# A transformer block on one core: four more units with a joint maximum step, value products and projections at other steps

## The chip, the cores and the metric

The kernel runs on one core of a Trainium2 chip. A core has five engines, each with its own instruction stream and working in order: TensorE (PE in the profile; PEld are its weight loads), VectorE (DVE), ScalarE (ACT), GpSimd (POOL) and SyncE (SP), which here only issues transfers. They meet through semaphores. Matrix products land in PSUM, eight banks of 128 partitions x 512 fp32 values, from which DVE and ACT read.

The metric is the device time of one execution in microseconds (us), as the median over several runs. A separate, profiled execution gives the trace.

## The reference

A layer-normed multi-head attention block, followed by a layer-normed gated feed-forward block, each with its residual. One sequence of 2048 tokens, width 512, 32 heads of 16, feed-forward width 1792, bf16 inputs.

```python
x = A_x                                              # 1 x 2048 x 512
h = x + A_ref(layernorm(x), A_wqkv, A_wo)
h2 = h + B_ref(layernorm(h), B_w_gate, B_w_up, B_w_down)

def A_ref(x, wqkv, wo):                              # H = 32, Dh = 16
    q, k, v = split_heads(x @ wqkv)
    scores = einsum("bhqd,bhkd->bhqk", q, k) * Dh ** -0.5
    p = softmax(scores, axis=-1)
    return merge_heads(einsum("bhqk,bhkd->bhqd", p, v)) @ wo

def B_ref(x, w_gate, w_up, w_down):
    return (gelu_tanh(x @ w_gate) * (x @ w_up)) @ w_down
```

The softmax needs the maximum of each of the 32 x 2048 rows of 2048 scores before the exponentials.

## The kernel before, in words

**Units and steps.** Attention is cut into 64 units: 8 groups of 256 queries (`gi`), and in each 8 slots of 4 heads. A unit's index is `ui`; units 8g to 8g+7 are group g. The schedule is written out by a planner in Python that runs through steps (`tick` in the code), 16 to a unit. Everything below is recorded into one list per engine, in the planner's order; the engines then run these lists, held up only by semaphores.

**First pass, for the maxima.** In each step PE computes two score tiles of 128 queries x 512 keys, of two heads (`p1_pair`, matmuls at line 825, 32 rows high since a head has 16 values and some room for the maximum), into a pair of PSUM banks. DVE reduces the pair to its maxima in one instruction over 128 x 1024 values (`p1_consume`, line 840, into `PM`). Two pairs of banks take turns. At the end of a unit POOL combines the maxima (`negm_part`, `negm_pre`), splits the negated maximum into three bf16 parts, SP transposes them (`STG`), and POOL adds them into the query tile `QT` (line 888), so that the second pass's scores come out with the maximum already taken off.

**Joint units.** In the units listed in `JOINT` two of the first pass's steps become one. For two heads, `item_diff` has PE compute the scores of the fourth block of 512 keys less those of the third (lines 1022 and 1024, the second with negated queries `QN` that POOL makes at line 1014), and ACT keeps the positive part (a Relu, line 1027, into `RB`, which shares the space of `OA`). At step 10 of the unit DVE adds this to the third block's scores and takes the maximum, with one instruction for each of the two heads (line 837): max(s3, s4) = s3 + max(s4 - s3, 0). Step 14 (`J_GONE`) then has nothing left to do and is left out altogether, for the second pass too, whose two tiles per step are made up for by a third tile in odd steps (`behind`).

**Second pass, for the probabilities.** It runs 24 steps behind the first (`P2_START`). In each step PE computes two tiles of 128 keys x 256 queries, twice (line 904), and ACT turns each 512 columns of PSUM into bf16 exponentials (`p2_consume`, line 933) in a ring of 34 tiles (`PTM`, `PTE`, `PTG`). It uses the banks 4 to 7, which it shares with the dense work. After the last step of the first pass the second goes on alone, two tiles to one ACT instruction (line 921).

**Dense work.** One queue (`Dense`) holds everything else that PE does, a piece in each step, behind the step's scores:
- `item_pv`: the products of the exponentials with the values, 64 matmuls a unit (line 947), in four pieces. A piece may start no earlier than its step in the unit's second pass; the list `PV_T` gives the first step, and in the kernel before the other three are `4 * p + 5`, so that they stand at 13, 14, 15 and 17. Then ACT copies the result (`OB`, line 669), SP transposes it, and POOL inverts the sums and multiplies (lines 981 and 985) into `Otok`.
- `post_onT` and `item_oproj`: when all slots of a group are done, SP transposes `Otok` into `OnT` (line 1067), PE projects it (line 1087) and adds the residual, ACT copies with a sum (line 1094), a Square with a sum follows (`sq`, line 1101), POOL finishes the layer norm, and SP transposes the result (`post_hnT`, line 1077). `clear` lets both transposes start in a window of a unit's steps only.
- `item_gate`, `item_up`, `item_down`: the feed-forward of 256 tokens: 7 pairs of gate and up, each with an ACT copy (line 669), a tanh on ACT (line 1148) and six POOL instructions, and two output projections of 14 matmuls (line 1220) and one for the residual (line 1225).

Where a step has too little dense work the planner fills with matmuls whose result nobody reads (`dummy`, line 1380). The planner keeps an account of how far ACT is behind (`act_lag`), and starts gate and up, output projections, difference items (`LAG_EXTRA`) and the Square (`LAG_OP`) only while it is small.

**The end.** The feed-forward of the last group can only follow the last attention unit (`tail_b`). There DVE takes over copies from ACT, and what dense work is left is put into waits (`fill`) or in front of the last feed-forward.

Of the kernel before, what the change touches and what calls it, by code (L numbers as in the profile page):

```python
# [218 lines left out]

NPT_M, NPT_E, NPT_G = 23, 4, 7  # L220
NPT = NPT_M + NPT_E + NPT_G
PV_T = (13, 14, 16, 17)
ADDX = 3
LAGX = 8
PAUSE = 1
# [4 lines left out]
LAG_OP = 0.2  # L230
TANH_LAG = 2
SLOPE = 0.02
JOINT = (12, 14, 17, 20, 25, 28, 33, 36, 41, 44, 49)
J_AT, J_GONE = 10, 14
LAG_EXTRA = 0.2
POLY = 1.3
TICK = 1.135
TOOK = {1.04: 1.13, 0.62: 0.7, 1.27: 1.26, 1.45: 1.67, 0.31: 0.4}
# [3 lines left out]
def bass_sequential_preLN__mha_block__geglu_ffn__prompt_kernel(nc, A_x, A_wqkv, A_wo, B_x, B_w_gate, B_w_up, B_w_down, out):  # L242
    dbg = None
    with ExitStack() as es:
# [268 lines left out]
        def startable(it, room):  # L513
            if it[0] is item_gate and par_busy[it[1][1] % 2] and room < 10:
                return False
            if it[0] is item_down and it[1] == (GL - 1, 1) and not force[0]:
                return False
            if it[0] is item_down and not force[0] and (tight() or dense.now // 16 in JOINT and dense.now % 16 > J_GONE - 6 or act_lag[0] > LAG_START):
                return False
# [4 lines left out]
        class Dense:  # L524
# [27 lines left out]
            def piece(self):  # L552
                if self.single and self.pause > 0:
                    return 0
                while True:
                    if self.gen is None:
# [6 lines left out]
                        elif self.prio and (not self.single or self.prio[0][3] <= self.now):  # L563
                            self._start(self.prio.pop(0))
                        elif self.extra and not tight() and act_lag[0] <= LAG_EXTRA and self.now + 2 <= lim and not (self.ready and self.ready[0][0] is item_up):
                            self._start(self.extra.pop(0))
# [26 lines left out]
        dense = Dense()  # L593
        behind = [0]
        def tight():
            return dense.now // 16 in JOINT and dense.now % 16 >= J_GONE - 2 or bool(behind[0])

        deferred = []
        def defer(k, fn):
            deferred.append((dense.now + k, fn))  # L600
        force = [False]
# [47 lines left out]
        act_lag = [0.0]  # L649
        def act_more(cost):  # L650
            act_lag[0] += cost
# [179 lines left out]
        def p1_consume(ui, tiles):  # L831
            par = ui % 2
            (b, qt, kc, g), (b2, _, _, g2) = tiles
            if ui in JOINT and (qt, kc, g) == (1, 2, 0):
                assert y_left[ui] == 0, "differences too late"
# [7 lines left out]
        def negm_part(ui, k):  # L843
# [10 lines left out]
            else:  # L854
# [3 lines left out]
                P.op("pool", lambda e: e.tensor_scalar(out=m3, in0=m3, scalar1=-1.0, scalar2=None, op0=ALU.mult), reads=[("MXm", par)], writes=[("MXm", par)])  # L858
                if ui in JOINT:
                    P.op("pool", lambda e: e.tensor_copy(out=PM[:, par, 1, 3, 0:2], in_=PM[:, par, 1, 2, 0:2]), reads=[("PM", par, 1, 2, g_) for g_ in (0, 1)], writes=[("PM", par, 1, 3, g_) for g_ in (0, 1)])  # L860
# [75 lines left out]
        def item_pv(b, ui):  # L936

            gi, slot = units[ui]
            for p in range(4):
                while not force[0] and dense.now < P2_START + 16 * ui + 4 * p + 5:  # L940
                    yield ("wait", 1)
                for m in (2 * p, 2 * p + 1):
                    for i in range(2):
                        kt = 2 * m + i
                        for g in range(4):
                            pi = pt_of[(ui, m, g)]
                            P.op("pe", lambda e, g=g, kt=kt, pi=pi, i=i: e.matmul(pbank[32 * g:32 * g + 17, b, 0:256], VA[:, kt, 4 * slot + g, :],  # L947
                                                                                  PTt(pi)[:, 256 * i:256 * i + 256], start=(kt == 0), stop=(kt == NT - 1), tile_position=(0, 32 * g)),
                                 reads=[("V", kt), "VA_ones", ("PT", pi)], writes=[("pb", b)], sig=(g == 3 and i == 1))
                    for g in range(4):  # L950
                        pt_busy.discard(pt_of.pop((ui, m, g)))
                if p < 3:
                    yield 2
            par, col = slot // 2 % 2, slot % 2
            if gi == GL and slot >= NSLOT - 2:
                evac_act(OA[:, par, 256 * col:256 * col + 256], pbank[:, b, 0:256], [("pb", b)], [("OA", par, col), ("RB", 1)], cost=0.27)
                if col == 0:
                    dense.add(item_ofin, gi, front=True, est=3, not_before=dense.now + 3)
            else:
                evac_act(OB[:, ui % 2, :], pbank[:, b, 0:256], [("pb", b)], [("OB", ui % 2)], cost=0.27, then=lambda: o_turn(ui))  # L960
            pv_done.add(ui)
            return 2

        pv_done = set()
        P2_START = 16 + LAGX

        ob_busy = {}
        def o_turn(ui):
            gi, slot = units[ui]
            par = ui % 2  # L970
            assert not ob_busy.get(par), "GpSimd too far behind"
            ob_busy[par] = True
            P.dma("sp", lambda e: e.dma_start_transpose(out=OBT[:, par, :, :], in_=OB[:, par, :]), ("obT", par), reads=[("OB", par)], writes=[("OBT", par)])
            o4 = OBT[:, par].rearrange("p q (g i) -> p q g i", i=32)
            defer(5, lambda: o_norm(gi, slot, par, o4, ("OBT", par), ob_busy))
# [25 lines left out]
            yield  # L1001

        def clear(fn):
            if not force[0] and not 5 <= dense.now % 16 <= 14:
                defer(1, lambda: clear(fn))
            else:
                fn()
# [36 lines left out]
        def add_ffn(gi):  # L1044
            for f in range(NFC // 2):
                dense.add(item_gate, gi, f, est=3)
                dense.add(item_up, gi, f, est=3)
            for k in range(2):
                dense.add(item_down, gi, k, est=5)

        def add_ffn_when(gi):
            if w_pieces or not qkv_over[0]:
                defer(1, lambda: add_ffn_when(gi))
            else:
                add_ffn(gi)
# [7 lines left out]
        def post_onT(gi, k):  # L1063
            gp = gi % 2
            if k == 0:
                load_xres(gi)
            P.dma("sp", lambda e: e.dma_start_transpose(out=OnT[:, k, :, :], in_=Otok[:, k, :]),
                  ("onT", k), reads=[("Otok", s_) for s_ in range(NSLOT)], writes=[("OH", k)])
            if k == 1:
                otok_consumed[gi] = True  # L1070
            dense.add(item_oproj, gi, k, front=True, est=3, not_before=dense.now + 4)

        hn_left = {}
        ffn_done = {}
        def post_hnT(gi, k):
            gp = gi % 2
            P.dma("sp", lambda e: e.dma_start_transpose(out=hnT_l[gp][:, :, 128 * k:128 * k + 128], in_=hn_sb[:, k, :]),
                  ("hnT", 2 * gp + k), reads=[("OH", k)], writes=[("hnT", gp, k)])
            hn_left[gi] = hn_left.get(gi, 2) - 1
            if hn_left[gi] == 0:  # L1080
                defer(3, lambda: add_ffn_when(gi))

        def item_oproj(b, gi, k):
            gp, t = gi % 2, 2 * gi + k
            hh = g_h(gi, k)
            for hc in range(4):
                P.op("pe", lambda e, hc=hc: e.matmul(pbank[:, b, :], OnT[:, k, hc, :], wo_sb[:, hc, :], start=(hc == 0), stop=False),
                     reads=[("OH", k), "wo"], writes=[("pb", b)], sig=False)
                if hc == 1:
                    yield 2  # L1090
            P.op("pe", lambda e: e.matmul(pbank[:, b, :], ident[:], hh, start=False, stop=True),
                 reads=["ident", ("h", gp, k)], writes=[("pb", b)], sig=True)
            act_more(0.48)
            P.op("act", lambda e: e.activation(out=hh, in_=pbank[:, b, :], func=ACT.Copy, accum_out=hsum[:, t:t + 1]),
                 reads=[("pb", b)], writes=[("h", gp, k), ("hsum", t)])
            def sq():
                if not force[0] and act_lag[0] > LAG_OP:
                    defer(1, sq)
                    return
                act_more(0.48)  # L1100
                P.op("act", lambda e: e.activation(out=hn_sb[:, k, :], in_=hh, func=ACT.Square, accum_out=hsq[:, t:t + 1]),  # L1101
                     reads=[("h", gp, k)], writes=[("OH", k), ("hsq", t)])
                defer(1, lambda: pool.add(ln2_from_sums(gi, k, t), then=lambda: defer(2, lambda: clear(lambda: post_hnT(gi, k)))))
            defer(2, sq)
            return 3
# [287 lines left out]
        tick = 0  # L1393
        J_ = sorted(JOINT)
        J_PREP = {max(160, 16 * (J_[i - 1] if i else 0) + 12): J_[i] for i in range(len(J_))}
# [7 lines left out]
        while True:  # L1403
            p1_ok = tick < 16 * NU
            if p1_ok and tick // 16 in JOINT and tick % 16 == J_GONE:
                for i, (k_, fn_) in enumerate(deferred):
# [68 lines left out]
            if p2_ok and t2 % 16 == 0:  # L1475
                dense.add(item_pv, t2 // 16, front=True, est=5, not_before=tick + PV_T[0])
            if doubles[0]:
# [61 lines left out]
```

## Time and profile before

| | |
|---|---|
| time, median of 3 runs | 1240.03 us (1239.23 to 1241.87) |
| time of the profiled execution | 1240.23 us |
| its span, first to last instruction | 1238.5 us |
| PE busy | 1099.2 us |
| DVE busy | 1182.2 us |
| ACT busy | 1196.3 us |
| POOL busy | 785.3 us |
| mean granted clock of TensorE | 0.997 |
| DVE maxima, 128 x 1024 (line 840) | 1002 of 1213 ns each |
| exponentials, 512 columns (line 933) | 2000, about 704 ns each |

The first pass takes from 14.7 to 1183.1 us of the span, the second alone to 1206.9, the end the rest. A duration in such a table is that of one instruction from its start to its end. Instructions of one engine overlap a little, so that the distance from one start to the next can be shorter than the duration.

### The profile page before, as it was taken

How to read it: one execution, taken by the hardware profiler on the slowest of the kernel's cores; microseconds unless marked ns; L12 is line 12 of the kernel's file. 1: busy time of each engine (PE TensorE's matmuls, PEld its weight loads, DVE VectorE, ACT ScalarE, POOL GpSimd, SP SyncE). 2: the span in 40 equal slices, each digit the busy share in tenths (PEclk: the TensorE clock that was granted, in tenths of full speed). 3: DMA queues.
4: the chain of work that ended last, by engine and by line, in shares of the span. 5: the costliest groups of instructions: out<-in, count | busy, mean ns of one | idle time of the engine just before them, and what ended most of it. 6: DMA issues, size and time to landing. Idle time of an engine off the chain costs nothing.

```text
span 1238.5 us, 31200 instructions
## 1 busy us (share of the span) xinstructions
PE 1099.2 (89%) x12389; PEld 429.3 (35%) x12588; DVE 1182.2 (95%) x1111; ACT 1196.3 (97%) x2433; POOL 785.3 (63%) x1624
## 2 busy tenths in 40 slices
PE   7898888888888999889988999989988898888888
PEld 3232222233333333333333333333333333323345
DVE  8999999999999999999999999999999999999933
ACT  7899999999999999999999999999999999999992
POOL 8555884455756467674667638574676847865781
PEclk9999999999999999999999999999999999999999
DMA  5111113400010001000010100100001000010000
GB/s 151 27 30 25 30 27 108 117 10 8 10 25 17 14 12 23 16 15 17 8 27 12 14 17 8 27 16 15 12 10 30 12 18 8 7 32 20 8 15 18
DMA packets 68656, 31.52 MB, mean 25 GB/s; under 512 B 53920, under 2 KB 67488, under 8 KB 68512
## 3 DMA queue, kind: packets, MB, share of 16 engines
q1 hardware_dynamic: 68512, 29.52, 9.9%
q8 instruction: 101, 1.65, 0.6%
q14 instruction: 43, 0.35, 0.1%
HBM read 11.80 MB, written 2.10 MB: 11 GB/s over the span
## 4 chain that ended last, share of the span: by engine, by line
ACT 59%; DVE 30%; PE 8%; issue 1%; POOL 1%; DMA 1%
ACT PTM L933 33%; DVE PM L840 29%; ACT PTG L933 10%; ACT PTE L933 6%; PE pbank L1220 2%; ACT th_sb L1148 2%; ACT u_sb L669 2%; ACT g_sb L669 1%; PE pbank L825 1%; ACT PTM L921 1%; PE pbank L904 1%; PE pbank L1380 1%; PE pbank L1168 1%; ACT OB L669 1%; ACT OnT L1101 1%
## 5 line engine op out<-in xcount | busy, mean ns | idle before, releaser
L840 DVE TENSOR_REDUCE PM<-pbank 128x2 f32<-128x1024 f32 x1002 | 1141.9, 1213 | 11.3 <-PE pbank L904 7.4
L933 ACT ACTIVATE PTM<-pbank 128x512 bf16<-128x512 f32 x1357 | 727.4, 704 | 6.6 <-PE pbank L904 2.0
L904 PE MATMUL pbank<-QT,KT 32*128 32x256 bf16 x4096 | 517.6, 273 | 17.8 <-ACT PTM L933 6.5
L825 PE MATMUL pbank<-KT,QT 32*128 32x512 bf16 x2026 | 390.5, 384 | 25.3 <-DVE PM L840 10.7
L1380 PE MATMUL pbank<-ones_bf,ident 128*128 128x512 bf16 x639 | 206.0, 384 | 65.0 <-ACT PTM L933 31.9
L933 ACT ACTIVATE PTG<-pbank 128x512 bf16<-128x512 f32 x407 | 227.6, 704 | 1.2
L825 PEld LDWEIGHTS pbank<-KT,QT 32*128 32x128 bf16 x2026 | 98.7, 91 | 367.6 <-DVE PM L840 134.4
L904 PEld LDWEIGHTS pbank<-QT,KT 32*128 32x128 bf16 x4096 | 171.5, 92 | 90.4 <-ACT PTM L933 47.2
L933 ACT ACTIVATE PTE<-pbank 128x512 bf16<-128x512 f32 x236 | 137.3, 700 | 0.6
L947 PE MATMUL pbank<-PTM,VA 128*17 128x256 bf16 x2776 | 126.0, 274 | 5.2 <-ACT PTG L933 1.1
L981 POOL TENSOR_TENSOR LINV<-OBT,negone 128x8 f32<-128x8 bf16 x62 | 103.4, 1667 | 0.0
L1380 PEld LDWEIGHTS pbank<-ones_bf,ident 128*128 128x128 bf16 x804 | 46.2, 97 | 137.4 <-ACT PTM L933 90.8
L947 PEld LDWEIGHTS pbank<-PTM,VA 128*17 128x17 bf16 x2776 | 59.9, 89 | 49.7 <-issue 29.8
L1158 POOL TENSOR_TENSOR th_sb<-g_sb 128x512 f32<-128x512 f32 x49 | 50.9, 1039 | 34.9 <-ACT g_sb L669 34.9
L868 POOL TENSOR_TENSOR MX<-PM,MX 128x8 f32<-128x8 f32 x64 | 12.8, 200 | 92.7 <-DVE PM L840 92.1
L1168 PE MATMUL pbank<-hnT_l,wg_sb 128*128 128x256 bf16 x448 | 66.6, 274 | 2.8 <-ACT PTG L933 0.2
L1168 PE MATMUL pbank<-hnT_l,wu_sb 128*128 128x256 bf16 x448 | 66.5, 275 | 2.8 <-ACT PTM L933 0.2
L888 POOL TENSOR_TENSOR QT<-QT,STG 128x256 bf16<-128x256 bf16 x64 | 42.7, 668 | 35.0 <-DMA STG<-ST 35.0
L1157 POOL TENSOR_TENSOR th_sb<-th_sb,g_sb 128x512 f32<-128x512 f32 x49 | 62.1, 1267 | 3.2
L1160 POOL TENSOR_TENSOR th_sb<-th_sb,g_sb 128x512 f32<-128x512 f32 x49 | 62.1, 1267 | 2.9
L1212 POOL TENSOR_TENSOR GUT<-th_sb,u_sb 128x512 bf16<-128x512 f32 x49 | 62.1, 1267 | 2.0
L855 POOL TENSOR_TENSOR MX<-PM,MX 128x8 f32<-128x8 f32 x64 | 12.9, 201 | 74.8 <-DVE PM L840 74.0
(164 smaller groups left out, 1138.6 us busy)
## 6 DMA issues: line engine op xcount, KB each, us to landing
QKS<-QKS SPq DMA_DIRECT2D x27, 112.0 KB, 2.1
x_sb<-in_A_x_dram SPq DMA_DIRECT2D x4, 512.0 KB, 5.6
xres<-in_A_x_dram SPq DMA_DIRECT2D x16, 128.0 KB, 2.3
out_dram<-out_sb SPq DMA_DIRECT2D x16, 128.0 KB, 1.7
wg_sb<-in_B_w_gate_dram SPq DMA_DIRECT2D x4, 448.0 KB, 4.0
wu_sb<-in_B_w_up_dram SPq DMA_DIRECT2D x4, 448.0 KB, 3.9
wd_sb<-in_B_w_down_dram SPq DMA_DIRECT2D x3, 512.0 KB, 5.0
STG<-ST SPq DMA_TRANSPOSE x64, 2.3
```

Source lines behind the costliest of these rows:

```text
L825: P.op("pe", lambda e, g=g, b=b: e.matmul(pbank[:, b, :], QT[32 * g:32 * g + 32, c, slot, 128 * qt:128 * qt + 128], KT[32 * g:32 * g + 32, ...
L840: P.op("dve", lambda e: e.tensor_reduce(out=PM[:, par, qt, kc, g:g + 2], in_=pbank[:, b:b + 2, :], axis=AX.X, op=ALU.max), reads=[("pb", b ...
L904: P.op("pe", lambda e, kt=kt, i=i: e.matmul(pbank[:, b, 256 * i:256 * i + 256], KT[32 * g:32 * g + 32, slot, 128 * kt:128 * kt + 128], QT[ ...
L933: P.op("act", lambda e, b=b, pi=pi: e.activation(out=PTt(pi), in_=pbank[:, b, :], func=ACT.Exp), reads=[("pb", b)], writes=[("PT", pi)], e ...
L947: P.op("pe", lambda e, g=g, kt=kt, pi=pi, i=i: e.matmul(pbank[32 * g:32 * g + 17, b, 0:256], VA[:, kt, 4 * slot + g, :], PTt(pi)[:, 256 * ...
L981: P.op("pool", lambda e: e.tensor_tensor(out=li, in0=o4[:, :, :, 16], in1=negone[:, 0:8].rearrange("p (q h) -> p q h", q=2), op=ALU.pow), ...
L1157: o(1.27, lambda e: e.tensor_tensor(out=ts_, in0=ts_, in1=gs, op=ALU.mult), [("th", par), ("g", par)])], then=done)
L1158: pool.add([o(1.04, lambda e: e.tensor_tensor(out=ts_, in0=gs, in1=gs, op=ALU.mult), [("g", par)], dE), o(0.62, lambda e: e.tensor_scalar( ...
L1160: o(1.27, lambda e: e.tensor_tensor(out=ts_, in0=ts_, in1=gs, op=ALU.mult), [("th", par), ("g", par)])], then=poly_done)
L1168: P.op("pe", lambda e, dc=dc, fc=fc, i=i: e.matmul(pbank[:, b, 256 * i:256 * i + 256], w[:, dc, 128 * fc:128 * fc + 128], hT[:, dc, :], st ...
L1212: P.op("pool", lambda e: e.tensor_tensor(out=o_ap, in0=shp(ts_), in1=shp(us), op=ALU.mult), reads=[("th", par), ("u", par)], writes=o_keys ...
L1380: P.op("pe", lambda e: e.matmul(pbank[:, b, :], ident[:], ones_bf[:, 0:512], start=True, stop=True), reads=["ident", "ones_bf"], writes=[( ...
```

## The change

1. `JOINT` has 15 units instead of 11: unit 12 goes, 11, 22, 30, 38 and 46 come.
2. The four pieces of the value products take their steps from `PV_T`, 15, 16, 17 and 18.
3. The window in which `clear` lets the transposes start ends at step 13 instead of 14.
4. `item_oproj` may start 5 steps after its transpose is issued instead of 4.
5. The feed-forward of a group is added 4 steps after its last transpose instead of 3.
6. The Square waits while a gate or up item is under way and ACT's account with it would be over the limit.
7. `LAG_EXTRA`, up to which a difference item may start, is 0.3 instead of 0.2.

The computation is the same.

```diff
-PV_T = (13, 14, 16, 17)
+PV_T = (15, 16, 17, 18)
...
-JOINT = (12, 14, 17, 20, 25, 28, 33, 36, 41, 44, 49)
+JOINT = (11, 14, 17, 20, 22, 25, 28, 30, 33, 36, 38, 41, 44, 46, 49)
 J_AT, J_GONE = 10, 14
-LAG_EXTRA = 0.2
+LAG_EXTRA = 0.3
...
             for p in range(4):
-                while not force[0] and dense.now < P2_START + 16 * ui + 4 * p + 5:
+                while not force[0] and dense.now < P2_START + 16 * ui + PV_T[p]:
                     yield ("wait", 1)
...
         def clear(fn):
-            if not force[0] and not 5 <= dense.now % 16 <= 14:
+            if not force[0] and not 5 <= dense.now % 16 <= 13:
                 defer(1, lambda: clear(fn))
...
-            dense.add(item_oproj, gi, k, front=True, est=3, not_before=dense.now + 4)
+            dense.add(item_oproj, gi, k, front=True, est=3, not_before=dense.now + 5)
...
-                defer(3, lambda: add_ffn_when(gi))
+                defer(4, lambda: add_ffn_when(gi))
...
             def sq():
-                if not force[0] and act_lag[0] > LAG_OP:
+                if not force[0] and act_lag[0] + (0.48 if dense.gen is not None and dense.cur in (item_gate, item_up) else 0) > LAG_OP:
                     defer(1, sq)
                     return
```

## The prediction

> **What bounds the kernel now.** I read the page's busy shares first, then the chain of waits.
>
> ```profile
> PE 1099.2 (89%) x12389; PEld 429.3 (35%) x12588; DVE 1182.2 (95%) x1111; ACT 1196.3 (97%) x2433; POOL 785.3 (63%) x1624
> ...
> ACT 59%; DVE 30%; PE 8%; issue 1%; POOL 1%; DMA 1%
> ```
>
> DVE and ACT are both nearly always busy and the chain changes between them, so neither line names the pace. "Busy" counts an instruction until it has left the engine, and successive ones overlap; the pace is the distance from start to start. The timeline of DVE around a joint step, then of ACT:
>
> ```profile
> 673.56 9.33 DVE L840 TENSOR_REDUCE PM<-pbank 128x2 f32<-128x1024 f32 x8 [0.21 <-PE pbank L904]
> 682.81 0.68 DVE L837 CUSTOM_DVE_ANT_0 OA<-pbank,OA 128x512 f32<-128x512 f32 x1
> ...
> 684.03 5.78 DVE L840 TENSOR_REDUCE PM<-pbank 128x2 f32<-128x1024 f32 x5
> ```
>
> ```profile
> 526.06 1.27 ACT L933 ACTIVATE PTG<-pbank 128x512 bf16<-128x512 f32 x2
> 527.01 0.81 ACT L669 ACTIVATE u_sb<-pbank 128x512 f32<-128x512 f32 x1
> 527.49 2.29 ACT L933 ACTIVATE PTM<-pbank 128x512 bf16<-128x512 f32 x4
> ```
>
> A plain DVE step is 1.131 us (the usual start-to-start distance of L840; its lasting 1.213 hides 0.08 of idling), the joint step 684.03 - 682.81 = 1.22. An exponential, or any 512-column copy from PSUM, holds ACT 0.477 us (526.06 to 527.01 is two); a tanh 0.52, the 256-column OB copy 0.264, a Square with its sum read 0.61, an oproj copy with its sum read 0.57. The windows show DVE alone setting the time, stretch by stretch:
>
> ```profile
> core 0: us, PE busy (x) PEld busy (x) DVE busy (x) ACT busy (x) POOL busy (x), PEclk, DMA share, GB/s
> 110.67:219.27 108.60, 92.15 (x1090) 30.83 (x1106) 108.60 (x98) 107.23 (x216) 73.45 (x130) 1.00 0.20 57
> 633.35:778.55 145.20, 131.41 (x1510) 50.94 (x1534) 143.81 (x133) 144.60 (x300) 93.44 (x198) 1.00 0.08 16
> 671.02:688.59 17.57, 15.64 (x181) 5.93 (x182) 17.27 (x20) 17.57 (x38) 14.66 (x33) 1.00 0.15 17
> 816.22:834.72 18.50, 16.58 (x181) 5.99 (x182) 17.41 (x20) 17.86 (x38) 14.67 (x33) 0.91 0.08 15
> ```
>
> Six units without a feed-forward take 108.60 = 6 x 18.10 = 96 x 1.131: DVE back to back, to the hundredth. A full group of 8 (units 34 to 41, joints 36 and 41) takes 145.20, where DVE needs 124 x 1.131 + 2 x 1.22 = 142.7: 2.5 us of DVE stalls. ACT needs in it, by its counts, 257 exponentials, 14 gate and up copies, 4 Relus and 2 output copies x 0.477 = 132.1, 7 tanh 3.6, 8 OB 2.1, 2 Squares 1.2, 2 oproj copies 1.1: 140.2. So DVE paces, ACT follows with 2 to 3% of room, and the stalls come where ACT's work lumps: PE waits for a bank that ACT still reads, and the next pair of scores, queued behind on PE, reaches DVE late.
>
> **The change part by part.** Sums are made against the profiled execution, 1240.23 us (span 1238.5, 1.7 around it); the median of the runs is 0.2 below it.
>
> *Four more joint units (11, 22, 30, 38, 46 in, 12 out).* Each takes two plain DVE steps, 2 x 1.131, and puts one of 1.22 in: -1.04. In the joint unit the step that goes is a step of the whole schedule. 4 x -1.04 = -4.2, on the pacing engine. Added per unit: two Relus (2 x 0.477 on ACT), four 32-row matmuls on PE less one pair of score matmuls, one POOL negation (0.55, POOL is 63% busy). On ACT a group's need becomes 140.7 (140.2 + 1.0, less one exponential that belongs to the next group), DVE's 122 x 1.131 + 3 x 1.22 = 141.6. DVE still needs more, by 0.9 us instead of 2.5. Ends: -4.2 in full, or nothing, if ACT's idle time cannot shrink. I take it in full, because the new units are those whose stalls were least: from the starts of DVE's steps, units 22, 30, 38 and 46 lost 0.10, 0.18, 0.18 and 0.18 us, against 0.5 to 0.9 in 26 to 28 and 34 to 36.
>
> By the Trainium skill (ScalarE: Activation LUTs, What ACT_TABLE_LOAD costs) an ACTIVATE with immediates takes 186 ns + 0.833 ns a column, and successive ones overlap by 93 ns: an estimate of 0.52 us at 512 columns. By that ACT would need 152 us a group, be the pace already, and each added Relu would cost its full time. The rows contradict it: 0.477 from PSUM, and the group took 145.2; 0.52 holds here for the tanh, which reads SBUF.
>
> *Where ACT's work falls (value products, the Square's condition, LAG_EXTRA, the later add of the feed-forward).* These add no instruction, they move them. I went through both programs' order step by step, set ACT's work of each step at the durations above against 1.131 us and carried what is left over. In before the remainder passes 0.7 us in 99 steps of units 2 to 62, in after in 40; its peaks in a group fall from 0.95, 1.38 and 1.03 (units 35 to 37) to 0.93, 0.72 and 0.72. The stalls before, without the two places named below, are 13.7 us: 3.8 in 693 steps with under 0.4 left over, 3.9 in 163 up to 0.7, 3.3 in 76 up to 1.0, 2.7 in 23 above. With the same stall per step of each class, the 720, 201, 37 and 3 steps of after give 3.9 + 4.8 + 1.6 + 0.4 = 10.7: -3.0. Ends: -5 (the upper classes' 6.0 all but gone) and +0.8 (no smoothing, and after each new joint the 0.2 us that units 15, 18, 29 and 37 lose behind one, while ACT takes three exponentials in odd steps). I take -3.0, since all its classes are measured.
>
> *Value products at 15, 16, 17, 18 instead of 13, 14, 15, 17.* 64 products a unit and their OB copy move; SP issues the OB transpose and POOL its inverse (1.67) and multiply (0.40) one step later; 17 inverses instead of 7 now stand behind the add that completes the next queries (L888, 0.67), on which they put nothing. The probability tiles are held longer: 34 tiles are reused after 17 steps, so the cover between product and next exponential shrinks from 4 steps to 2, still 2.3 us. On PE four runs of 16 products now stand in successive steps; a step with such a run went 316.23 to 317.21 = 0.98 us when PE was not held up, under 1.131. Nothing, with the third rival as its bad end.
>
> *Projection one step later; no transposes at step 14.* One stall bears on it:
>
> ```profile
> 1085.17 3.31 DMA OnT<-Otok
> 1088.48 0.05 issue
> 1088.53 0.60 PE pbank L1087 x2
> ```
>
> PE stood 1.75 us before this projection, and DVE's step behind it came 1.15 late. One step more (1.13) covers that: -1.1. Ends: 0 (the transpose is later by as much) and -2 (the steps behind it, at half clock, recover too). The other 13 projections waited for no transfer; a step later costs them nothing, and a transpose that step 14 would have issued goes seven steps later: the feed-forward has its group to run in. What is late next there is ACT.
>
> *The end.* The build leaves less for it: all 49 gate and up copies are on ACT before the second pass is alone (before, two gates and three ups were left), so both output projections of group 6 are out of the way early. Before, the second stood in front of the last feed-forward:
>
> ```profile
> 1214.28 0.38 PE pbank L1225
> 1214.65 2.37 PE pbank L1220 x11
> 1217.03 0.22 PE pbank L1225
> 1217.24 5.24 PE pbank L1168 x48
> ```
>
> 11 matmuls and one more go, 2.6 us; the last feed-forward now waits for hnT, whose copies end at 1214.7: 2.4 saved. Against it one run of products falls behind the last scores: 16 products and 3 fillers (1.1 us) into the 1.0 us that PE idles there, 1204.5 to 1206.9, waiting for exponentials; with some margin 0.3 lost. -2.1; ends -2.6 and 0 (if the earlier projection holds up the score pairs there).
>
> Sum: -4.2 - 3.0 - 1.1 - 2.1 = -10.4: 1229.8, so a median of 1229.6.
>
> **The rivals.**
> 1. *Joints pay, stalls do not shrink.* Lumps of after may stall as much at a lower height; 5.8 of the 13.7 us came with less than 0.7 left over and without lump (u15 lost 0.18 at 0.42). -4.2 + 0.8 - 1.1 - 2.1: 1233.6.
> 2. *ACT becomes the pace.* ACT idled 145.2 - 140.2 = 5.0 us a group. If that cannot shrink, a joint only adds its Relus: 4 x 0.95 = 3.8, less 3.2 for projection and end: 1240.8, no change. Against it: stretches with less to do lie beside the lumps, and after fills them more evenly.
> 3. *PE becomes the pace in the run of products: slower.* Place: steps 15 to 18 of each of 62 units. Each pays 4 x (x - 1.131), x being PE's step. At x = 1.18 the loss is 12 us and eats everything; at 1.25, 29 us: 1259 and more. For it: PE is busy 131.4 of 145.2. Against it: fillers are in that, and 0.98 is the row.
> 4. *More half-clock stretches.* Twice the granted clock was about 0.5 for 3.4 us (820.4 to 823.8, 1090.1 to 1093.5), after PE had waited. Units 36 and 44 hold the same work; 44 met one and took 18.50 against 17.57: 0.93 each. The difference matmuls stand where full-height fillers stood (804 before, 772 after). Four more: 1233.5. The Trainium skill (TensorE: Matmul & The Clock Gate, Part 1) says that the clock halves when the array was too little busy in a free-running window of about 3.4 us; the trace agrees in the length, 3.413 us.
>
> **How the numbers follow.** Forecast 0.58, rival 1 0.18, rival 2 0.08, rival 3 0.06, rival 4 0.07; 0.03 for what I do not see. The range goes from 1226.0 (stalls at their good end, -5, with the end at -2.6, and a half-clock stretch spared) to 1237.0, between rivals 1 and 2; outside it lie rivals 2 and 3 and a little of the rest. 0.2%, 2.5 us, is about what this kernel's runs can tell from no change. Faster: forecast, rivals 1 and 4, some of the rest: 0.85; rival 2 and neighbours same: 0.06; slower: 0.09.
>
> **What would show it.** Right: joint units of 17.1 to 17.4 us at 22, 30, 38 and 46; groups of 143 to 144; no wait of PE for OnT; no L1220 between the OnT transposes of the end and the last L1168; DVE still at 1.131. Wrong: plain units of 18.5 and more behind the joints with ACT back to back (rival 2), score pairs more than 1.131 apart in the product steps without a wait for ACT or DVE (rival 3), or a clock under 1 in many windows (rival 4).

## The result, and the profile after

The changed kernel takes 1237.26 us (median of 8 runs, 1235.99 to 1238.76) against 1240.03 (1239.23 to 1241.87, 8 runs): ratio 0.9973, 95% interval 0.9963 to 0.9983. It is faster, by 2.8 us (0.3%) instead of the 10.4 forecast, and lies 0.3 us above the range. The profiled execution took 1235.99 us, its span is 1234.3. Its runs with a granted clock of 1.0 took 1236.0 to 1237.0 us, those with 0.996 to 0.998 1237.5 to 1238.8.

Busy shares and chain of waits, from the page of the changed kernel:

```profile
PE 1106.0 (90%) x12428; PEld 430.4 (35%) x12564; DVE 1176.2 (95%) x1115; ACT 1196.7 (97%) x2445; POOL 787.7 (64%) x1632
...
ACT 66%; DVE 15%; PE 9%; POOL 6%; issue 3%; DMA 0%; POOLq 0%; DVEq 0%
```

DVE is busy 6 us less, but the chain went from DVE (30% to 15%) to ACT (59% to 66%): more often than before, DVE waits for something that ACT set. The windows of the same kind as before, six units without a feed-forward and units 34 to 41:

```profile
core 0: us, PE busy (x) PEld busy (x) DVE busy (x) ACT busy (x) POOL busy (x), PEclk, DMA share, GB/s
110.83:219.43 108.60, 91.44 (x1094) 30.25 (x1106) 108.60 (x97) 106.52 (x214) 69.38 (x126) 1.00 0.23 68
635.07:779.80 144.73, 130.84 (x1506) 49.61 (x1520) 142.91 (x136) 144.15 (x299) 88.01 (x194) 1.00 0.07 16
```

DVE still runs at 1.131 us a step where nothing disturbs it (108.60 = 96 x 1.131). The group with three joints instead of two should have lost 1.04 us against 145.20 by the joint alone, and lost 0.47.

For the account that follows, a *stall* is the distance from the start of one DVE maximum to that of the next, less 1.131 us (1.22 behind a joint step), added up from unit 2 on. The *end* is the span less the end of the first pass.

| kernel | joints | first pass ends | stalls | of them at steps 7 and 8 | at steps 9 and 10 | end |
|---|---|---|---|---|---|---|
| before | 11 | 1183.1 | 16.7 | 4.0 | 1.0 | 55.4 |
| changed | 15 | 1181.3 | 19.2 | 0.5 | 9.1 | 52.9 |

So the joints saved their 4.2 us, the stalls gave 2.4 back, and the end is 2.5 shorter: 4.2 us in all, which is the difference of the two spans. The 9.1 us stand in one place: steps 9 and 10 of a unit are the third and fourth of the four steps in which the value products now run (7 to 10 of a unit of the first pass, 15 to 18 of the second). In the kernel before the products stood at 5, 6, 7 and 9, and its 4.0 us at steps 7 and 8 have the same place among them. One of these stalls in unit 33 of the changed kernel, from the timeline of all engines (start, duration, engine, line, and in brackets the idle time before it and what ended it):

```profile
624.96 0.39 PE L825 MATMUL pbank<-KT,QT 32*128 32x512 bf16 x2
...
625.39 0.95 ACT L1148 ACTIVATE th_sb<-th_sb 128x512 f32<-128x512 f32 x1
...
625.91 3.40 ACT L933 ACTIVATE PTM<-pbank 128x512 bf16<-128x512 f32 x6
...
625.94 0.39 PE L825 MATMUL pbank<-KT,QT 32*128 32x512 bf16 x2
...
626.89 0.39 PE L904 MATMUL pbank<-QT,KT 32*128 32x256 bf16 x2 [0.55 <-ACT PTM L933]
...
627.20 0.61 PE L947 MATMUL pbank<-PTM,VA 128*17 128x256 bf16 x16
...
627.75 0.39 PE L825 MATMUL pbank<-KT,QT 32*128 32x512 bf16 x2
...
628.18 1.23 DVE L840 TENSOR_REDUCE PM<-pbank 128x2 f32<-128x1024 f32 x1 [0.41 <-PE pbank L904]
```

A PE step with products takes 0.98 us (624.96 to 625.94) when nothing holds it up. Behind the tanh the second pass's tile waits until 626.88 for a bank that ACT still reads. The products follow it, and the next first-pass pair comes at 627.75, 1.81 us after the one before. DVE stands 0.41 us. In 30 of the 49 feed-forward pairs ACT is given the tanh in step 14 or 15 of the second pass (6 or 7 of the first pass's unit), just ahead of the products or in their first step. The 36 units with a tanh or a Square in these two steps hold 8.9 of the 9.1 us, the other 26 hold 0.2. Before, 15 tanh and 4 Squares stood in the corresponding steps, 4 and 5, and these 19 units hold 3.6 of the 4.0 us.

The projection's transfer was waited for again, longest in unit 26 (SP's own timeline, then PE's weight loads and DVE in that of all engines):

```profile
502.05 1.17 SPq L973 DMA_TRANSPOSE OBT<-OB  x1
503.26 1.57 SPq L1060 DMA_DIRECT2D xres<-in_A_x_dram  x2
504.88 1.19 SPq L1067 DMA_TRANSPOSE OnT<-Otok  x1
```

```profile
507.44 0.11 PEld L1087 LDWEIGHTS pbank<-wo_sb,OnT 128*128 128x128 bf16 x2 [1.76 <-DMA OnT<-Otok]
...
508.41 1.23 DVE L840 TENSOR_REDUCE PM<-pbank 128x2 f32<-128x1024 f32 x1 [0.90 <-PE pbank L904]
```

The transpose went out behind an OB transpose and the residual's loads on SP, 2.56 us before PE had its result, and DVE lost 0.98. The end, PE's timeline:

```profile
1208.63 2.54 PE L1220 MATMUL pbank<-wd_sb,GUT 128*128 128x512 bf16 x11
1211.00 0.38 PE L1225 MATMUL pbank<-xres,ident 128*128 128x512 bf16 x1
1211.68 0.72 PE L1305 MATMUL pbank<-ident,OnT 128*128 128x128 bf16 x8
1212.24 0.59 PE L1225 MATMUL pbank<-xres,ident 128*128 128x512 bf16 x2
1212.85 1.03 PE L1168 MATMUL pbank<-hnT_l,wg_sb 128*128 128x256 bf16 x8
```

The eleven output matmuls that stood in front of the last feed-forward now run before the transposes for it (L1305). The feed-forward starts 4.4 us earlier (1217.24 before), 2.6 of them not from the first pass.

### The profile page after: what moved, and what is told of

The parts are those of the page before. It is cut to its first block, busy times and chain, and to the rows that moved or that the text cites. A ratio compares the mean times of both kernels' runs of the same rounds, so it can differ in the third digit from the quotient of the medians.

```text
span 1234.3 us, 31289 instructions
## 1 busy us (share of the span) xinstructions
PE 1106.0 (90%) x12428; PEld 430.4 (35%) x12564; DVE 1176.2 (95%) x1115; ACT 1196.7 (97%) x2445; POOL 787.7 (64%) x1632
## 4 chain that ended last, share of the span: by engine, by line
ACT 66%; DVE 15%; PE 9%; POOL 6%; issue 3%; DMA 0%; POOLq 0%; DVEq 0%
ACT PTM L933 38%; DVE PM L840 15%; ACT PTG L933 12%; ACT PTE L933 6%; PE pbank L1220 3%; ACT g_sb L669 2%; ACT u_sb L669 2%; ACT th_sb L1148 2%; PE pbank L904 1%; PE pbank L825 1%; ACT OA L1027 1%; ACT OB L669 1%; PE pbank L1168 1%; POOL th_sb L1158 1%; POOL th_sb L1157 1%
## 5 line engine op out<-in xcount | busy, mean ns | idle before, releaser
L1380 PE MATMUL pbank<-ones_bf,ident 128*128 128x512 bf16 x668 | 208.9, 383 | 54.5 <-ACT PTM L933 27.4
L904 PEld LDWEIGHTS pbank<-QT,KT 32*128 32x128 bf16 x4096 | 175.3, 92 | 98.0 <-ACT PTM L933 57.0
L1220 PE MATMUL pbank<-wd_sb,GUT 128*128 128x512 bf16 x213 | 57.9, 382 | 2.8 <-ACT OB L669 1.3
L868 POOL TENSOR_TENSOR MX<-PM,MX 128x8 f32<-128x8 f32 x64 | 12.8, 201 | 69.2 <-DVE PM L840 68.9
```

Source lines behind the costliest of these rows:

```text
L904: P.op("pe", lambda e, kt=kt, i=i: e.matmul(pbank[:, b, 256 * i:256 * i + 256], KT[32 * g:32 * g + 32, slot, 128 * kt:128 * kt + 128], QT[ ...
L1220: P.op("pe", lambda e: e.matmul(pbank[:, b, :], GUT[:, fc, 128 * k:128 * k + 128], wd_sb[:, fc, :], start=first, stop=last), reads=[("GUT" ...
L1380: P.op("pe", lambda e: e.matmul(pbank[:, b, :], ident[:], ones_bf[:, 0:512], start=True, stop=True), reads=["ident", "ones_bf"], writes=[( ...
```

## Experiments

All times are medians, ratios are to the kernel before on the same chip, with their 95% interval; stalls are those of one trace each. Diffs are against the changed kernel unless another is named. The text calls a kernel by the first part of its name, e3 for e3_eleven_joints.

| kernel | time us | ratio | joints | first pass ends | stalls | steps 9, 10 | end |
|---|---|---|---|---|---|---|---|
| e2_products_alone | 1239.95 | 1.0000 (0.9991 to 1.0009) | 11 | 1185.1 | 18.7 | 5.2 | 52.4 |
| e3_eleven_joints | 1234.78 | 0.9959 (0.9945 to 0.9972) | 11 | 1180.5 | 14.2 | 6.3 | 52.5 |
| e3s_tanh_kept_out | 1247.58 | 1.0059 (1.0046 to 1.0072) | 11 | 1180.2 | 13.4 | 4.4 | 65.8 |
| e7_products_14_17 | 1253.68 | 1.0109 (1.0094 to 1.0124) | 15 | 1176.2 | 14.0 | 3.8 | 73.7 |
| x1_short_relus | 1236.44 | 0.9967 (0.9955 to 0.9980) | 15 | 1181.8 | 19.5 | 8.8 | 52.9 |
| x7_no_tanh_at_run | 1225.73 | 0.9886 (0.9873 to 0.9900) | 15 | 1171.6 | 9.3 | 1.5 | 52.9 |
| x8_no_tanh_elsewhere | 1233.43 | 0.9945 (0.9932 to 0.9959) | 15 | 1178.5 | 16.2 | 7.7 | 51.9 |
| j13_thirteen_joints | 1235.10 | 0.9965 (0.9951 to 0.9978) | 13 | 1180.8 | 16.5 | 7.4 | 52.4 |
| j12_twelve_joints | 1236.63 | 0.9968 (0.9956 to 0.9979) | 12 | 1181.8 | 16.4 | 6.7 | 52.0 |
| j6_six_joints | 1236.11 | 0.9968 (0.9956 to 0.9981) | 6 | 1182.8 | 10.1 | 5.3 | 52.0 |
| x4_projection_4 | 1233.84 | 0.9948 (0.9934 to 0.9961) | 11 | 1179.7 | 13.2 | 8.9 | 52.4 |
| x5_products_back | 1268.59 | 1.0228 (1.0214 to 1.0242) | 11 | 1181.1 | 14.2 | 2.2 | 85.7 |
| y1_half_products | 1260.60 | 1.0168 (1.0153 to 1.0183) | 15 | 1205.8 | 43.5 | 4.5 | 52.8 |
| y2_pair_before_products | 1256.80 | 1.0134 (1.0114 to 1.0154) | 15 | 1202.2 | 39.0 | 0.04 | 53.0 |
| y3_eleven_pair_before | 1253.45 | 1.0111 (1.0096 to 1.0126) | 11 | 1200.0 | 32.5 | 0.02 | 52.4 |
| y4_eleven_pair_before_all | 1253.93 | 1.0113 (1.0098 to 1.0128) | 11 | 1199.0 | 32.9 | 13.5 | 53.0 |

In e7 and x5 the products stand earlier, and the corresponding steps are 8 and 9 (5.5 us in e7) and 7 and 8 (4.4 us in x5).

**Which part does what.** The products alone, on the kernel before:

```diff
-PV_T = (13, 14, 16, 17)
+PV_T = (15, 16, 17, 18)
-                while not force[0] and dense.now < P2_START + 16 * ui + 4 * p + 5:
+                while not force[0] and dense.now < P2_START + 16 * ui + PV_T[p]:
```

> The kernel before with one part of the change: the value products at steps 15, 16, 17, 18; everything else, 11 joints too, as before. Theory A (the run of products, with three banks left for the scores, collides with a tanh or Square that ACT does just before or in it; each such meeting costs DVE 0.1 to 0.5 us at steps 9 and 10 of a unit): 30 such meetings in this order instead of 19 before, so about 6 to 8 us of DVE stalls at steps 9 and 10, first pass 2 to 4 us longer than before, the end about 2.4 shorter as in the changed kernel: 1239.5 to 1242. Theory B (the product steps are harmless; the new joints did not pay because ACT sets the pace): no stalls of note at steps 9 and 10, first pass not longer, end 2.4 shorter: 1236 to 1238.

As theory A had it, with stalls at steps 9 and 10 somewhat lower (5.2 us): the later products cost the first pass 2.0 us and win 3.0 at the end; the time is the same. The end's gain comes with this part alone. Then everything but the joints (e3), with the list of the kernel before:

```diff
-JOINT = (11, 14, 17, 20, 22, 25, 28, 30, 33, 36, 38, 41, 44, 46, 49)
+JOINT = (12, 14, 17, 20, 25, 28, 33, 36, 41, 44, 49)
```

> The changed kernel with the 11 joint units of before. Theory A: the joints paid in full (4 x 1.04 = 4.2), less the meetings that go with them (30 instead of 37, 0.25 each, 1.8): 2 to 4.2 us slower than the changed kernel, 1239.3 to 1241.5. Theory B (ACT sets the pace): as fast as the changed kernel or up to 3 us faster, 1234 to 1237.5.

Theory A missed, and the time is B's: without the four new joints the kernel is not slower. The medians differ by 2.5 us, but the two 95% intervals overlap, and at a granted clock of 1.0 the two spans differ by 1.4. The joints save 4.2 us of DVE steps and bring 5.0 of stalls, 2.8 of them at steps 9 and 10. The same with other lists (13 joints: without 30 and 38; six: 12, 17, 25, 33, 41, 49; twelve: the old list and 22):

> The changed kernel with 13 joint units: without 30 and 38. Theory R: between 11 joints (1234.8) and 15 (1237.3), 1235 to 1236.5. If instead single joints are good or bad by their place, it falls outside: under 1234.5 (30 and 38 were the bad ones) or over 1237 (they were the good ones).

> The changed kernel with 6 joint units (12, 17, 25, 33, 41, 49). Theory R: five joints fewer than in the kernel with eleven give back 5 x 1.04 = 5.2 us and spare 1 to 3 us of stalls, since ACT then has room: 1237 to 1239. If joints never pay under this order of the dense work: 1232 to 1234.5.

> e3_eleven_joints with unit 22 as a twelfth joint, the one whose group lost least in the changed kernel. If a joint's worth depends on its place (1.04 saved, 0.2 more stalls in group 2): 1233.7 to 1234.7. If a further joint costs about what it saves wherever it stands: 1234.7 to 1235.7.

From 6 to 11, 13 and 15 joints a further one brought 0.82, 1.15 and 1.36 us of stalls against the 1.04 it saves; unit 22 alone, as a twelfth, brought 2.2, of which 0.8 is the wait for the projection's transfer at unit 26: the traces with unit 22 in the list have it (0.8, 0.8 and 1.0 us), those of e3 and j6 do not. The thirteen came within what was expected, the six between the two views (1236.11 us), the twelve above both. Each figure rests on one trace a kernel, and the lists differ in place too. As far as they go, a joint pays less the more there are, and behind the eleventh none won anything.

**Is it the Relus' time on ACT?** In the new joints 22, 30, 38 and 46 they were cut to 16 columns:

```diff
-            P.op("act", lambda e: e.activation(out=RB[:, g, :], in_=pbank[:, b, :], func=ACT.Relu), reads=[("pb", b)], writes=[("RB", g)], extra_deps=dG)
+            w = 16 if ui in (22, 30, 38, 46) else 512
+            P.op("act", lambda e: e.activation(out=RB[:, g, 0:w], in_=pbank[:, b, 0:w], func=ACT.Relu), reads=[("pb", b)], writes=[("RB", g)], extra_deps=dG)
```

> The changed kernel, same order of instructions on every engine, with the Relus of the joint units 22, 30, 38 and 46 cut from 512 columns to 16 (the other 496 columns of the difference are not refreshed, so the maxima of these units are not the right ones). ACT is spared 8 x about 0.4 = 3.2 us; DVE, PE and POOL do the same work. Theory R (ACT's room: each further joint adds 0.95 us of Relus and takes 1.04 us of time from a group where ACT has some 4 us left, and what does not fit comes back as DVE stalls): the stalls fall by 2 to 4 us, first pass to 1177.5 to 1179.5, time 1233 to 1235.5. Theory S (the joints hurt by pushing the dense work to worse steps; the Relus' time itself does not matter): stalls fall by under 1 us, time 1236 to 1237.5.

Theory R falls: a short Relu lasts 254 ns on average against 682 for a whole one, some 3 us in all, and the stalls are 19.5 us against 19.2. Of S it is shown that the Relus' time is not it. That the joints push dense work to worse steps was not tested; what fits it is that 36 units of the changed kernel have a tanh or a Square in steps 6 and 7, and 28 of e3.

**Is it the tanh at the products?** The tanh given to ACT in steps 14 and 15 of the second pass left out, and as a counterpart all others. The expectations count 29 and 20; in the traces 30 are missing in x7 and 19 in x8.

```diff
+                if (dense.now - P2_START) % 16 not in (14, 15):      # x8: in (14, 15)
                 P.op("act", lambda e: e.activation(out=ts_, in_=ts_, func=ACT.Tanh, scale=GC), reads=[("th", par)], writes=[("th", par)])
```

> The changed kernel, same order otherwise, without the 29 tanh that ACT is given at steps 14 and 15 of a unit's second pass, just before and in the product run (the gelu of these tiles is left out; their polynomial goes on unchanged). ACT is spared 29 x 0.52 = 15 us. Theory A (the meeting of tanh and product run): the DVE stalls at steps 9 and 10 fall from 9.1 to under 2.5 us, those of other steps (10.1) by little, first pass 1172 to 1175, time 1228 to 1231. Theory C (four product runs in succession by themselves): stalls at steps 9 and 10 stay over 6 us, time 1234 to 1237.

> The counterpart of x7: the changed kernel, same order, without the 20 tanh at all steps but 14 and 15 of a unit's second pass (the gelu of these tiles is left out). ACT is spared 10 us, as general room. Theory A (the meeting of tanh and product run): the stalls at steps 9 and 10 stay at 7.5 us or more (9.1 in the changed kernel). Rival D (it was ACT's room at large, not the place, that x7 gave back): they fall to 6 or below. Time by A 1232.5 to 1236.5, by D 1229 to 1232.

Theory A holds in both, though x7 came out 2 us below its range. The 30 took 9.9 us of stalls with them (0.33 each), 7.6 of it at steps 9 and 10; the other 19 took 3.0 (0.16 each), and 7.7 us stayed at steps 9 and 10. The group of DVE's maxima on the pages of the kernel before and of the changed one (busy, mean; idle before, and who ended most of it), then the chain's shares and the same group on the page of the kernel without the 30:

```profile
L840 DVE TENSOR_REDUCE PM<-pbank 128x2 f32<-128x1024 f32 x1002 | 1141.9, 1213 | 11.3 <-PE pbank L904 7.4
```

```profile
L840 DVE TENSOR_REDUCE PM<-pbank 128x2 f32<-128x1024 f32 x994 | 1134.0, 1214 | 12.4 <-PE pbank L904 8.5
```

```profile
ACT 49%; DVE 38%; PE 9%; issue 2%; POOL 1%; DMA 0%; SPq 0%; POOLq 0%; DVEq 0%
...
L840 DVE TENSOR_REDUCE PM<-pbank 128x2 f32<-128x1024 f32 x994 | 1130.0, 1219 | 7.3 <-PE pbank L904 4.7
```

DVE's share of the chain goes from 15% to 38%. A removed tanh is also time given to ACT, so 0.16 of the 0.33 may be that; the rest is where it stood.

**Can the tanh or the products simply go elsewhere?** The tanh kept from those steps by the planner (on e3), the products one step earlier (on the changed kernel), and the products at 13, 14, 15, 17 again (on e3):

```diff
-                if not force[0] and tight():
+                if not force[0] and (tight() or (dense.now - P2_START) % 16 in (14, 15, 0)):
```

```diff
-PV_T = (15, 16, 17, 18)
+PV_T = (14, 15, 16, 17)      # x5, on e3: (13, 14, 15, 17)
```

> As e3_eleven_joints, and the planner puts no tanh at steps 14, 15 and 16 of a unit's second pass, that is just before the product run or in its first half. Same instructions, same product steps. Theory A: the meetings fall from 30 to 10, the DVE stalls at steps 9 and 10 from some 7 to 2 or 3 us: first pass 4 to 5 us shorter than in e3_eleven_joints. More dense work is left for the end (up to 2.5 us): 1235 to 1238. Theory C (four runs of products in succession hold PE up by themselves, whatever ACT does): stalls at steps 9 and 10 as in e3_eleven_joints, time the same or up to 2.5 longer.

> The changed kernel with 15 joints, value products one step earlier (14, 15, 16, 17). Theory A: 31 meetings instead of 37, so 1 to 2 us less of stalls (now at steps 8 and 9), but more dense work left for the end (2.4): 1236.5 to 1239. Theory C (succession alone): same stalls as in the changed kernel, only one step earlier, 1238 to 1240.

> e3_eleven_joints with the value products back at 13, 14, 15 and 17. The planner then leaves more dense work for the end (536 PE instructions recorded there instead of 452). If that is what the product steps are for, the first pass gets shorter (1175 to 1180, fewer meetings: 17 instead of 30) and the end longer by far more (65 to 75 us instead of 52.5): 1245 to 1256. If the product steps only cost stalls, the end stays within 3 us of 52.5 and the time falls to 1231 to 1235.

None of the three is faster, and all three came out 9 us and more above everything expected. The first passes came out shorter or within 0.6 us of the same (1176.2 to 1181.1), and the end 13 to 33 us longer. In the last of the three, waits of DVE:

```profile
DVE GUT L1197 <- PE pbank L1168: 39.2, 7, 29.4
```

One wait of 29.4 us for the last feed-forward: dense work that no longer found its place beside the attention ran after it, and four half-clock stretches of 3.4 us fell there too. The steps of the products decide less about stalls than about how much is left for the end.

**The projection.** On e3:

```diff
-            dense.add(item_oproj, gi, k, front=True, est=3, not_before=dense.now + 5)
+            dense.add(item_oproj, gi, k, front=True, est=3, not_before=dense.now + 4)
```

> e3_eleven_joints with the projection 4 steps after its transpose instead of 5. By the prediction's reading PE waits for OnT again: 2 to 5 us of such waits in all (0.5 or less with 5 steps), 0.5 to 2.5 us slower than e3_eleven_joints (1234.8): 1235.3 to 1237.3. If the transfer is hidden anyway: no such waits, 1234 to 1235.2.

With the projection back at 4 steps no wait for `OnT` is left at all, and the time is 1233.84, below what was expected. The later projection is not what keeps the transfer hidden. This is the fastest version that does the whole work; its distance to e3 is less than both intervals. At steps 9 and 10 it loses 2.7 us more than e3 and at all others 3.7 less: one place alone does not tell the time.

**How the tanh reaches DVE.** Two theories: that 16 products stand between the freed bank and the next pair (W), or that the wait for the bank is itself the whole delay (K). Half of the products are left out (y1); then the next pair is put in front of them (y2); this with eleven joints and the projection at 4 (y3); and then in every step (y4). The edits of y1 and y2:

```diff
-                    for i in range(2):
+                    for i in range(1):
...
```

```diff
+            if p2_ok and p1_ok and not doubles[0] and not p1_next and (tick - P2_START) % 16 in (15, 0, 1, 2):
+                p1_next.append(p1_pair((tick + 1) // 16, (tick + 1) % 16, 1 - gp1))
             if doubles[0]:
```

> Leaves out half of the value products (the odd key blocks, 32 of 64 matmuls a unit); ACT, DVE and SP keep their lists, POOL its work, the product item holds its bank for the same steps. Theory W: a tanh makes PE wait for a bank in the run of products, and DVE stalls because 16 products then stand between the freed bank and the next score pair. With 8 products in their place DVE's stalls at steps 9 and 10 of the units fall from 9.1 us to under 5, and the time to 1231 to 1234.5. Theory K: it is the bank alone, whatever PE does behind it: the stalls there stay over 7.5 us, time 1235 to 1238.

> The changed kernel, with the first pass's next score pair put on PE ahead of the step's 16 products instead of behind them, in the four product steps of each unit; nothing is left out. Theory W: the delay reaches DVE only through the products that stand in front of the pair; DVE's stalls at steps 9 and 10 fall from 9.1 us to under 5, time 1230 to 1234.5. Theory K: the pair is as late behind the second pass's tile that waits for its bank; stalls there over 7.5 us, time 1235 to 1239.

> The same reordering on the kernel with eleven joint units and the projection 4 steps after its transpose (1233.8 us, 8.9 us of stalls at steps 9 and 10). Theory W: 1229 to 1232.5. Theory K: 1233 to 1236.

> As before it, but in every step the first pass's next pair stands ahead of the step's dense work. If every DVE stall reaches DVE through the dense work that stands in front of the pair, those at the other steps (4.2 us) shrink too: 1226 to 1231. If the stalls elsewhere have another way to DVE, it stands where the reordering of the product steps alone stands, within 1.5 us.

On the stalls of steps 9 and 10 W holds: 4.5 us with half of the products, 0.04 with the pair in front. On the time of y1, y2 and y3 both theories missed, by 17 us and more; y4 stands where its second view had it, 0.5 us beside y3. With the pair in front, 18.8 us turn up in y2 at steps 12 and 13 (0.5 in the changed kernel), 0.30 a unit. In unit 33 the start of step 12 comes 1.58 us behind the one before, on DVE:

```profile
639.76 1.22 DVE L840 TENSOR_REDUCE PM<-pbank 128x2 f32<-128x1024 f32 x1
641.34 3.49 DVE L840 TENSOR_REDUCE PM<-pbank 128x2 f32<-128x1024 f32 x3 [0.36 <-PE pbank L904]
```

There the order returns to the old one, and two pieces of dense work lie between two pairs in PE's list. Units 2 to 9, which have no tanh, lose 0.15 us each there too, so about half of the 18.8 us is the change of order itself. The 36 units with a tanh or a Square in steps 6 and 7 lose 0.37 on average, the other 26 lose 0.21: part of what the tanh cost is paid here. Another 8.3 us more than in the changed kernel stand at steps 0 to 3, and for them no cause was looked for. In front in every step (y4), each pair again has one piece between it and the last, and 13.5 us are back at steps 9 and 10, 12.2 of them in the 33 units with a tanh or a Square in steps 6 and 7. I read it so that the sum counts: PE's work of a product step and the wait behind the tanh together exceed 1.131 us, and an order can only choose where that shows. Why this last version loses 7.2 us at step 15 stays open.

With half of the products PE's time was not won, because the clock went. Windows of that kernel, in its unit 34:

```profile
core 0: us, PE busy (x) PEld busy (x) DVE busy (x) ACT busy (x) POOL busy (x), PEclk, DMA share, GB/s
649.50:653.80 4.30, 4.12 (x36) 1.48 (x36) 4.30 (x5) 4.30 (x10) 2.69 (x3) 1.00 0.04 8
653.80:655.50 1.70, 0.96 (x17) 0.34 (x14) 1.70 (x3) 1.70 (x5) 0.62 (x1) 1.00 0.00 0
655.50:657.20 1.70, 1.70 (x28) 0.57 (x26) 1.70 (x2) 1.70 (x5) 1.53 (x4) 0.93 0.02 5
657.20:660.60 3.40, 3.40 (x29) 1.05 (x26) 3.15 (x4) 3.35 (x9) 1.76 (x4) 0.50 0.10 22
660.60:664.00 3.40, 3.40 (x18) 0.53 (x16) 2.78 (x3) 3.12 (x8) 1.08 (x4) 0.53 0.47 118
```

After a stretch in which PE was busy 0.96 of 1.70 us, its clock is half for two stretches of 3.4 us, and DVE loses 0.87 of 6.8 us. The mean clock was 0.947: (1 - 0.947) x 1258.6 x 2 = 133 us at half clock, some 39 such stretches. By the trace's record of the clock, 22 of the 25 runs of them in the first pass begin in step 9 or 10 of a unit, among the thinned products, and 31 of the 43.5 us of stalls lie in them or in the step just behind.

## Why the prediction was right or wrong

**What bounds the kernel: right.** DVE at 1.131 us a step, the plain stretches equal to the hundredth.

**Where the error lies.** The forecast of the stalls was 16.7 - 3.0 - 1.1 = 12.6; measured were 19.2. This 6.6 us is the whole error against the profiled time (1229.8 + 6.6 - 0.4 at the end = 1236.0). Added in the order of the experiments, the products alone brought +2.0 (e2 less before; forecast nothing), all else but the joints -4.5 (e3 less e2; forecast -3.0 and -1.1), the four joints +5.0 (the changed kernel less e3; forecast nothing). Another order could divide it otherwise.

**Four joints, -4.2: right in the unit, failed at "I take it in full".** By size this is the larger failed step. Units 22, 30, 38 and 46 took 17.17, 17.47, 17.35 and 17.06 us, as forecast or 0.1 beside it, but the first pass became 0.8 us longer with them instead of 4.2 shorter. Of the 5.0 us of stalls 2.8 stand at steps 9 and 10, 1.0 is the wait for the projection's transfer at unit 26, which comes with unit 22 in the list, and the rest is spread. The reason given, that the new units had stalled least before, looked at the unit and not at what a joint does around it. Relu time is not it (x1); why each further joint brings more stalls stays open.

**ACT's lumps smoothed, -3.0: won in part outside the products, not in them.** Outside steps 7 to 10, and without the single long waits for a projection's transfer and the half-clock stretches behind them, the stalls were 8.8 us before, 9.9 in e2, 7.7 in e3 and 8.6 in the changed kernel. From e2 to e3 that is -2.2. That all parts but the joints and the products gave -4.5, so near to the forecast -4.1, is in part luck: 3.1 us of it is one such wait, in unit 34 of e2, that is not there in e3. At steps 7 to 10 the stalls rose from 4.9 to 9.6 us. Reckoned again from the order of ACT's instructions in the two traces, 202 of these steps had under 0.4 us left over and lost 8.7 us; before, 205 had and lost 2.7. The class knows how much ACT is behind, not what PE has still to do when ACT frees the bank. The classes also hang on the third digit: with 0.477 us for an exponential 50 steps of the kernel before pass 0.7, with 0.480 109 do.

**Product steps, "Nothing": the other step that failed.** The 0.98 us was a row in which PE was not held up, and the margin to 1.131 is 0.15. A tanh given to ACT just before holds PE up longer than that. Stalls of this kind were in the trace before, 4.0 us at steps 7 and 8, and were counted there as ACT's lumps. In the changed kernel they are 9.1 us at steps 9 and 10, and 36 units instead of 19 have a tanh or a Square just ahead. x7 brings them to 1.5, y2 to 0.04 at that place. It is the third rival in a milder form: not every product step paid, as its 12 us at 1.18 assumed, only those behind a tanh or a Square. The two cases were weighed as all or nothing; that they add up, a short margin and a hold-up in the same step, was no case at all.

**The projection, -1.1: not won.** The wait of the one group went, and another took its place at unit 26 (1.76 us on PE, 0.98 on DVE), where the transpose was issued behind other transfers on SP; "one step more covers that" counted steps from a planned issue. x4 needs no later projection.

**The end, -2.1: right**, with 2.5 measured, for the reason given; e2 shows that it comes with the products.

**Rival 4, more half-clock stretches: a small part.** The profiled execution had none in the first pass, two fewer than before, and yet some of the runs show them: 0.996 to 0.998 and 1 to 2 us. That is most of the difference between its profiled time and the median. y1 shows that taking matmuls out brings such stretches, none in the changed kernel's first pass and 39 in its own, at a price of 20 us and more. By the Trainium skill (TensorE: Matmul & The Clock Gate, Part 1) the default is the throttled clock and activity releases it. The windows above agree in that the half clock follows a stretch with little PE work; that it lasted a second stretch of 3.4 us behind one with PE busy all the time (3.40 of 3.40) they do not explain.

## What to carry to other kernels

An in-order engine with 13% of room in a step (0.98 of 1.131) has room for itself, not for a wait in front of its work: where a change puts several such steps in a row, look up what the engine that frees its buffers is given just before them. A saving on the pacing engine is not worth its full price of itself; here the twelfth to fifteenth joint brought more stalls than they saved, for a reason that stays open in part, and an intermediate version (eleven joints, the projection at 4 steps, the rest of the change, 1233.8 us) was faster than both kernels. And where work is planned into free places, moving it may decide less about the place it comes from than about what is left over at the end (1253.7 and 1268.6 us).

## What the runs showed of the hardware that was not expected

Taking matmuls away made the kernel slower: with 32 of 64 products a unit left out, PE's mean granted clock fell from 1.0 to 0.947, and the time rose from 1237.3 to 1260.6 us.

Relus of 16 instead of 512 columns in four units, some 3 us less for an engine that is busy 97%, moved neither stalls nor time beyond the noise (1236.44 us, stalls 19.5): a busy share of 97% on ACT did not mean that its time lacked in these steps. Where the work stood counted: the 30 tanh of steps 14 and 15 took 0.33 us of stalls each, the other 19 took 0.16.
